# Regrouping linear attention so that the values are never formed, with half the residual parked in DRAM

## The chip, the cores and the metric

The kernel runs on one core of a Trainium2 chip. Of the engines named below, TensorE does the matmuls, and VectorE, ScalarE and GpSimd the work element by element; SBUF and PSUM are memories on the chip, and matmuls write to PSUM. The metric is the device time of one execution in microseconds (us), the lowest being best. Every time below is a median of several executions. Ratios are the mean time of one kernel's runs over that of the other kernel's runs in the same rounds, so a ratio isn't quite the ratio of the medians quoted beside it. The kernel before moved between 1643.9 and 1644.4 us from one set of rounds to the next; differences below half a microsecond between sets are therefore not read.

## The reference, cut to what matters

Four layers on 2048 tokens of width 1024: attention, feed-forward, attention, feed-forward, each with a layer norm in front and a residual around it. The attention is linear, with 32 heads of 32:

```python
q, k, v = ...                                  # slices of layernorm(x) @ wqkv, per head
phi = lambda t: jnp.where(t > 0, t + 1, jnp.exp(t)) + 1e-6
pq, pk = phi(q), phi(k)
kv  = jnp.einsum("bhsd,bhse->bhde", pk, v)     # summed over all 2048 tokens
z   = jnp.einsum("bhsd->bhd", pk)
num = jnp.einsum("bhqd,bhde->bhqe", pq, kv)
den = jnp.einsum("bhqd,bhd->bhq", pq, z)[..., None] + 1e-6
return (num / den) @ wo
```

The feed-forward layers (width 3584, relu(gate) times up, then down) are most of the time and aren't changed.

## The kernel before: the parts concerned

Tokens are 16 tiles of 128, in four quarters of four tiles. A "unit" is one projection of one token tile onto 512 columns: eight matmuls into one of four PSUM buffers. Whatever has to happen some units later is put on a list (`later.at(n, f)`), which `tick()` works off after each unit; in two stretches the order of the instructions on VectorE, ScalarE or GpSimd is exactly the order in which they are written (`manual_schedule`).

```python
def phi(self, ps, out):                        # keys: 1 ScalarE pass, 2 VectorE instructions
    nc.scalar.activation(out=e, in_=ps, func=ACT.Exp)
    nc.vector.tensor_scalar(out=e, in0=e, scalar1=1.0, scalar2=1e-6, op0=ALU.min, op1=ALU.add)   # "min-and-add"
    nc.vector.scalar_tensor_tensor(out=out, in0=ps, scalar=0.0, in1=e, op0=ALU.max, op1=ALU.add) # "join"
# q_unit: queries instead take three ScalarE passes (Relu, Exp, + 1e-6) and the join

def kv_step(t):                                # kv += phi(K_t)^T V_t, per group of 4 heads
    for g in range(G):
        nc.tensor.matmul(kv[b][:, ...], lhsT=pk[t][:, g * P:(g + 1) * P],
                         rhs=va[t][:, g * P:(g + 1) * P], ...)

def z_mult(pq, sc, j):                         # denominator: a GpSimd product, then z_sum
    nc.gpsimd.tensor_tensor(out=prod, in0=pq, in1=zrow, op=ALU.mult); later.at(2, z_sum)
def z_sum(...):                                # VectorE: sum per head, + 1e-6, reciprocal; then z_scale
def z_scale(...):                              # GpSimd: phi(Q) times 1/den, then a DMA transpose

def fold_wo(i):                                # T = kv @ wo, 16 single matmuls of 512 columns
    ps = ...                                   # even i: 2 PSUM buffers, copied by VectorE
    nc.tensor.matmul(ps, lhsT=kvT[:, g, :], rhs=wo[:, g, :])
    (nc.scalar.activation if g % 2 else nc.vector.tensor_copy)(T[...], ps)
... (cut)
run(q2[:6])
run([with_fold(u, i) for i, u in enumerate(q2[6:] + q3[:6])])   # one unit, two folds, one unit, ...
```

Of the kernel before, what the change touches and what calls it, by code (L numbers as in the profile page):

```python
# [12 lines left out]
P = 128  # L13
NW = 512
HD = 32
QT = 4

# [61 lines left out]
class _Net:  # L79
    def __init__(self, tc, ctx, x_d, wqkv_d, wo_d, wg_d, wu_d, wd_d, out_d):  # L80
# [30 lines left out]
        self.kvp = pool("kvp", 1, space=PSUM)  # L111
        self.ring = _Ring(nc, self.wring, 5)
        self.later = _Later()

# [16 lines left out]
        self.xnT = {}  # L131
# [24 lines left out]
    def ln_norm(self, layer, t):  # L156
        nc = self.nc
        src = self.xb[t] if layer == 0 else self.x[t]
        stats = self.small.tile([P, 2, nc.vector.BN_STATS_DIM], F32, tag="stats")
        for c in range(2):  # L160
            self.ln_stat(t, src, c, stats)
        xn = self.ln_scale(src, *self.ln_rstd(stats))
        return xn

    def head(self):
# [10 lines left out]
        k0, k1, v0, v1 = (ring.place() for _ in range(4))  # L176
        self.load_x(0, 0)
        self.load_x(0, 1)
        v0(0, H)
        self.load_x(1)  # L180
        v0(H, 2 * H)
        self.load_x(2)
        v1()
        self.load_x(3)
        k0()
# [4 lines left out]
        k1()  # L190
        for t in range(8, self.ST):
            self.load_x(t)
        ring.load_to(5)
# [16 lines left out]
        with tc.manual_schedule(engines={mybir.EngineType.DVE, mybir.EngineType.Activation}):  # L210
            for j in range(QT):
                for c in range(2):
                    self.ln_stat(j, src[j], c, stats[j])
                r = self.ln_rstd(stats[j])
                xn = self.xnp.tile([P, self.D], BF16, tag="xn")
                for h in (0, 1) if j == 0 else (None,):
                    self.ln_scale(src[j], *r, xn, h)
                for h in range(2):
                    turn(j, xn, h)
# [9 lines left out]
    def ln_at(self, delay, layer, t, lag):  # L229
        def norm():  # L230
            xn = self.ln_norm(layer, t)
            self.later.at(lag, lambda: self.ln_turn(layer, t, xn))

        self.later.at(delay, norm)
# [5 lines left out]
    def phi(self, ps, out):  # L240
        nc = self.nc
        e = self.ep.tile([P, NW], F32, tag="e")
        nc.scalar.activation(out=e, in_=ps, func=ACT.Exp)  # L243
        nc.vector.tensor_scalar(out=e, in0=e, scalar1=1.0, scalar2=1e-6, op0=ALU.min, op1=ALU.add)  # L244
        nc.vector.scalar_tensor_tensor(out=out, in0=ps, scalar=0.0, in1=e,  # L245
                                       op0=ALU.max, op1=ALU.add)
# [7 lines left out]
    def plan_A(self, l):  # L254
        D = self.D
        cols = {"k0": D, "k1": D + NW, "v0": 2 * D, "v1": 2 * D + NW, "q0": 0, "q1": NW}
        for n in ("k0", "k1", "v0", "v1", "q0", "q1", "o0", "o1"):
# [6 lines left out]
    def layer_A(self, l, last_ln):  # L264
# [4 lines left out]
        pk, va, pq_of, pqT, T = {}, {}, {}, {}, []  # L269
# [4 lines left out]

        def slab_of(t):
            if t not in pk:
                s = self.slab.tile([P, 2, D], BF16, tag="slab", name=f"pkv{l}_{t}")
                pk[t], va[t] = s[:, 0, :], s[:, 1, :]
# [9 lines left out]
        def k_unit(q, j, c):  # L288
            t = q * QT + j
            slab_of(t)  # L290
            self.phi(project(f"k{c}", q, j), pk[t][:, c * NW:(c + 1) * NW])
            if c == H - 1:
                later.at(1, lambda: k_sum(t))

        def k_sum(t):
            if t == 0:
                nc.gpsimd.tensor_copy(out=ksum, in_=pk[t])  # L297
            else:
                nc.gpsimd.tensor_tensor(out=ksum, in0=ksum, in1=pk[t], op=ALU.add)  # L299

        def v_unit(q, j, c):
            t = q * QT + j
            slab_of(t)
            nc.scalar.activation(out=va[t][:, c * NW:(c + 1) * NW], in_=project(f"v{c}", q, j),
                                 func=ACT.Copy)

        def kv_step(t):

            for g in range(G):
                b, i = divmod(g, NW // P)  # L310
                nc.tensor.matmul(kv[b][:, i * P:(i + 1) * P], lhsT=pk[t][:, g * P:(g + 1) * P],  # L311
                                 rhs=va[t][:, g * P:(g + 1) * P], start=(t == 0 and i == 0),
                                 stop=(t == self.ST - 1 and i == NW // P - 1),
                                 skip_group_check=True)

        def z_row():

            hi = self.xnp.tile([P, D], BF16, tag="xn")
            nc.scalar.activation(out=hi, in_=ksum, func=ACT.Copy)
            for i in range(H):  # L320
                ps = self.ps3.tile([P, NW], F32, tag="b")
# [3 lines left out]

        def finish_kv():
            kvm = self.slab.tile([P, G, P], BF16, tag="slab", name=f"kvm{l}")
            for b in range(H):
                n = NW // P
                nc.vector.tensor_tensor(out=kvm[:, b * n:(b + 1) * n, :],  # L330
# [3 lines left out]
            nc.sync.dma_start_transpose(out=kvT, in_=kvm[:, :, :].rearrange("p g e -> p (g e)"))  # L334


        def q_unit(sc, j, c, lag):
            if j == 0 and c == 0:
                pqT[sc] = self.xnTp.tile([P, KT, QT * P], BF16, tag="xnT", name=f"pqT{l}_{sc}")
            if c == 0:  # L340
                pq_of[sc, j] = self.xnp.tile([P, D], BF16, tag="xn", name=f"pq{l}_{sc}_{j}")
            pq = pq_of[sc, j]
            ps = project(f"q{c}", sc, j)

            e = self.ep.tile([P, NW], F32, tag="e")
            nc.scalar.activation(out=e, in_=ps, func=ACT.Relu, scale=-1.0)  # L346
            nc.scalar.activation(out=e, in_=e, func=ACT.Exp, scale=-1.0)  # L347
            nc.scalar.activation(out=e, in_=e, func=ACT.Identity, bias=self.eps6[:, 0:1])  # L348
            nc.vector.scalar_tensor_tensor(out=pq[:, c * NW:(c + 1) * NW], in0=ps, scalar=0.0,  # L349
                                           in1=e, op0=ALU.max, op1=ALU.add)  # L350
            if c == H - 1:
                later.at(lag, lambda: z_mult(pq, sc, j))

        def z_mult(pq, sc, j):
            prod = self.prodp.tile([P, D], F32, tag="prod")
            nc.gpsimd.tensor_tensor(out=prod, in0=pq, in1=zrow, op=ALU.mult)  # L356
            later.at(2, lambda: z_sum(pq, prod, sc, j))

        def z_sum(pq, prod, sc, j):
# [4 lines left out]
            later.at(2, lambda: z_scale(pq, den, sc, j))  # L364

        def z_scale(pq, den, sc, j):
            nc.gpsimd.tensor_tensor(  # L367
                out=heads(pq), in0=heads(pq),
                in1=den[:, :].unsqueeze(2).to_broadcast([P, D // HD, HD]), op=ALU.mult)
            nc.sync.dma_start_transpose(out=pqT[sc][:, :, j * P:(j + 1) * P], in_=pq)  # L370
# [33 lines left out]
        def q_of(sc, lag):  # L404
            return [lambda j=j, c=c: q_unit(sc, j, c, lag) for j in range(QT) for c in range(H)]

        def out_of(sc):
            return [lambda j=j, c=c: out_unit(sc, j, c) for j in range(QT) for c in range(H)]

        def v_then_kv(q):  # L410
            u = column_major(v_unit, q)

            def last(j):
                u_j = u[QT + j]
                return lambda: (u_j(), later.at(2, lambda: kv_step(q * QT + j)))

            return u[:QT] + [last(j) for j in range(QT)]

        def k_then_kv(q):
            u = column_major(k_unit, q)  # L420

            def last(j):
                u_j = u[QT + j]
                return lambda: (u_j(), later.at(4, lambda: kv_step(q * QT + j)))

            return u[:QT] + [last(j) for j in range(QT)]
# [16 lines left out]
        first = column_major(v_unit, 0)  # L443
        if l == 0:

            first = [first[c * QT + j] for c, j in ((0, 0), (0, 1), (1, 0), (0, 2), (1, 1), (1, 2),
                                                    (0, 3), (1, 3))]
        def quarter0():
            run(first)
            run(k_then_kv(0))  # L450

        if l == 0:
            with self.tc.manual_schedule(engines={mybir.EngineType.DVE,mybir.EngineType.Activation}):
                quarter0()
        else:
            quarter0()
        run(column_major(v_unit, 1))
        run(k_then_kv(1))
        run(column_major(k_unit, 2))
        k3 = column_major(k_unit, 3)  # L460
        run(k3[:QT])
        ring.free_before((l, "k1"))
        run(k3[QT:])
        with self.tc.manual_schedule(engines={mybir.EngineType.DVE,mybir.EngineType.Pool}):
            ring.free_before((l, "v0"))
            later.at(5, z_row)
            run(q_of(0, 5), v_then_kv(2))
            run(q_of(1, 1), v_then_kv(3))
            ring.free_slowly((l, "q0"), later, 4)
            later.at(2, finish_kv)  # L470
            q2, q3, out0 = q_of(2, 1), q_of(3, 1), out_of(0)
# [4 lines left out]
            run(q2[:6])  # L476
            run([with_fold(u, i) for i, u in enumerate(q2[6:] + q3[:6])])
            run(q3[6:], out0[:2])
            run(out0[2:])
            ring.free_slowly((l, "o0"), later, 4)  # L480
            self.ln_later(last_ln, 0, 5, 4, 3)
            for sc in range(1, self.NQ):
                run(out_of(sc))
# [12 lines left out]
    def layer_B(self, l, final):  # L496
        nc, KT, D = self.nc, self.KT, self.D
        ring, later = self.ring, self.later
        for q in range(self.NQ):
# [22 lines left out]
            for n2 in range(D // NW):  # L522
# [6 lines left out]
                for dg in range(4):  # L529
                    ring.free_before((l, q, "d", n2, dg))  # L530
                    wd = ring.get((l, q, "d", n2, dg))
                    for j in range(QT):
# [3 lines left out]
                        for i, ps in enumerate(parts):  # L536
# [6 lines left out]
                            if dg == 3:  # L543
                                self.add_down(t, n2 * NW + i * n, ps[:, 0:n], final)
                        later.tick()
# [68 lines left out]
```

## Time and profile before

| | before |
|---|---|
| median | 1644.4 us |
| profiled span | 1642.1 us |
| TensorE waits, all rows | 5.6 us |
| of these, folding of wo | 1.5 us |
| kv matmuls (128 columns) | 256 |
| first projection, first gate of layer 2, first gate of layer 4 begin at | 7.49, 245.22, 1058.76 us |

TensorE works through nearly all of the span, so time is the number of matmuls times their spacing, plus holes. The views that show this stand in the prediction. One more: what VectorE does while wo is folded. Columns of a timeline are start, duration, engine, line, operation, output and inputs; in brackets the idle time before it and who ended it.

```profile
176.18 0.68 DVE L384 CAST T<-fold 128x512 bf16<-128x512 f32 x1
176.78 1.21 DVE L361 TENSOR_REDUCE den<-prod 128x32 f32<-128x1024 f32 x1
...
178.51 0.63 DVE L349 SCALAR_TENSOR_TENSOR pq<-ps,e 128x512 bf16<-128x512 f32 x1
179.06 0.68 DVE L384 CAST T<-fold 128x512 bf16<-128x512 f32 x1
```

And GpSimd in the same stretch:

```profile
175.22 1.92 POOL L367 TENSOR_TENSOR pq<-pq,den 128x1024 bf16<-128x1024 bf16 x1
178.07 2.13 POOL L356 TENSOR_TENSOR prod<-pq,zrow 128x1024 f32<-128x1024 bf16 x1 [0.93 <-DVE den L361]
```

### The profile page before, as it was taken

How to read it: one execution, taken by the hardware profiler on the slowest of the kernel's cores; microseconds unless marked ns; L12 is line 12 of the kernel's file. 1: busy time of each engine (PE TensorE's matmuls, PEld its weight loads, DVE VectorE, ACT ScalarE, POOL GpSimd, SP SyncE). 2: the span in 40 equal slices, each digit the busy share in tenths (PEclk: the TensorE clock that was granted, in tenths of full speed). 3: DMA queues.
4: the chain of work that ended last, by engine and by line, in shares of the span. 5: the costliest groups of instructions: out<-in, count | busy, mean ns of one | idle time of the engine just before them, and what ended most of it. 6: DMA issues, size and time to landing. Idle time of an engine off the chain costs nothing.

```text
span 1642.1 us, 18601 instructions
## 1 busy us (share of the span) xinstructions
PE 1625.1 (99%) x7632; PEld 749.7 (46%) x7786; DVE 577.7 (35%) x931; ACT 371.1 (23%) x699; POOL 195.6 (12%) x102
## 2 busy tenths in 40 slices
PE   8999999999999999999999999999999999999999
PEld 4444444444444444444444444444444444444444
DVE  6954876122211321222146457842112112211111
ACT  3356602101110110111033675121011101101110
POOL 0355800000000000000013566000000000000000
PEclk9999999999999999999999999999999999999999
DMA  8313726456445544644530146374544464455442
GB/s 251 57 52 82 180 41 172 148 168 191 154 137 169 156 151 157 187 150 138 168 76 1 58 104 154 56 201 145 176 144 153 159 198 150 144 158 163 154 160 71
DMA packets 298052, 227.18 MB, mean 138 GB/s; under 512 B 103152, under 2 KB 296048, under 8 KB 297968
## 3 DMA queue, kind: packets, MB, share of 16 engines
q1 hardware_dynamic: 293216, 221.80, 46.4%
q10 hardware_dynamic: 4752, 4.20, 0.8%
q8 instruction: 61, 1.00, 0.2%
q14 instruction: 23, 0.19, 0.0%
HBM read 197.13 MB, written 4.19 MB: 123 GB/s over the span
## 4 chain that ended last, share of the span: by engine, by line
PE 95%; ACT 2%; issue 1%; DVE 1%; DMA 1%; SPq 0%; ACTq 0%
PE pu L515 23%; PE pg L515 23%; PE acc L539 23%; PE ps L284 17%; PE ps L390 7%; PE kv L311 1%; DMA x<-in_A_x_dram 1%; ACT e L347 1%; ACT e L346 1%; PE acc_last L539 0%; DVE den L361 0%; ACT e L348 0%; DVE pq L349 0%; PE fold L378 0%; SPq L251 0%
## 5 line engine op out<-in xcount | busy, mean ns | idle before, releaser
L515 PEld LDWEIGHTS <-t 128*128 128x128 bf16 x3584 | 350.5, 98 | 423.1
L515 PE MATMUL pu<-xnT,t 128*128 128x512 bf16 x1756 | 420.2, 379 | 2.0
L515 PE MATMUL pg<-xnT,t 128*128 128x512 bf16 x1756 | 419.9, 379 | 1.7
L539 PE MATMUL acc<-t,hT 128*128 128x512 bf16 x1728 | 380.6, 379 | 2.0
L521 DVE TENSOR_TENSOR hT<-pu,rg 128x512 bf16<-128x512 f32 x224 | 154.7, 690 | 572.0 <-PE pu L515 553.5
L284 PE MATMUL ps<-t,xnT 128*128 128x512 bf16 x1500 | 338.1, 379 | 2.4 <-DVE xnT L206 0.3
L520 ACT ACTIVATE rg<-pg 128x512 f32<-128x512 f32 x224 | 133.6, 596 | 737.5 <-PE pg L515 708.8
L539 PEld LDWEIGHTS <-hT 128*128 128x128 bf16 x1820 | 177.9, 98 | 209.1
L284 PEld LDWEIGHTS <-xnT 128*128 128x128 bf16 x1536 | 148.6, 98 | 174.9 <-issue 1.6
L390 PE MATMUL ps<-T,pqT 128*128 128x512 bf16 x502 | 110.6, 379 | 0.5
L143 ACT ACTIVATE rstd<-mv,eps 128x1 f32<-128x1 f32 x64 | 18.8, 294 | 344.0 <-DVE mv L141 344.0
L297 POOL CAST ksum<-pkv 128x1024 f32<-128x1024 bf16 x2 | 2.1, 1036 | 682.3 <-DVE pkv L245 682.3
L554 DVE TENSOR_TENSOR xo<-x,acc 128x512 bf16<-128x512 f32 x31 | 21.3, 688 | 170.0 <-PE acc L539 170.0
L136 DVE BATCH_NORM_STATS2 stats<-x 128x6 f32<-128x512 f32 (+1 forms) x120 | 78.2, 672 | 1.8 <-DMA x<-in_A_x_dram 1.1
L390 PEld LDWEIGHTS <-pqT 128*128 128x128 bf16 x512 | 50.1, 98 | 60.4
L356 POOL TENSOR_TENSOR prod<-pq,zrow 128x1024 f32<-128x1024 bf16 x32 | 68.0, 2126 | 58.2 <-DVE den L361 35.8
L551 DVE TENSOR_TENSOR x<-x,acc 128x512 f32<-128x512 f32 x32 | 21.7, 677 | 149.5 <-PE acc L539 148.4
L299 POOL TENSOR_TENSOR ksum<-ksum,pkv 128x1024 f32<-128x1024 f32 x30 | 65.0, 2167 | 69.6 <-DVE pkv L245 68.2
L244 DVE TENSOR_SCALAR e<-e 128x512 f32<-128x512 f32 x64 | 54.6, 853 | 40.8 <-ACT e L243 40.8
L349 DVE SCALAR_TENSOR_TENSOR pq<-ps,e 128x512 bf16<-128x512 f32 x64 | 42.9, 670 | 68.3 <-ACT e L348 68.2
L367 POOL TENSOR_TENSOR pq<-pq,den 128x1024 bf16<-128x1024 bf16 x32 | 61.2, 1912 | 10.5 <-issue 4.0
L243 ACT ACTIVATE e<-ps 128x512 f32<-128x512 f32 x64 | 37.7, 596 | 66.4 <-PE ps L284 65.3
(46 smaller groups left out, 490.1 us busy)
## 6 DMA issues: line engine op xcount, KB each, us to landing
t<-in_B_W_gate_dram SPq DMA_DIRECT2D x56, 1024.0 KB, 6.5
t<-in_B_W_up_dram SPq DMA_DIRECT2D x56, 1024.0 KB, 5.3
t<-in_B_W_down_dram SPq DMA_DIRECT2D x64, 896.0 KB, 5.1
t<-in_A_wqkv_dram SPq DMA_DIRECT2D x11, 1024.0 KB, 5.1
t<-in_A_wo_dram SPq DMA_DIRECT2D x4, 1024.0 KB, 5.1
out_dram<-xo ACTq DMA_DIRECT2D x31, 128.0 KB, 2.2
x<-in_A_x_dram SPq DMA_DIRECT2D x15, 256.0 KB, 8.0
t<-in_A_wqkv_dram SPq DMA_DIRECT2D x2, 512.0 KB, 4.9
```

The source lines that it names most:

```text
L136: self.nc.vector.bn_stats(out=stats[:, c, :], in_=src[:, c * fmax:(c + 1) * fmax])
L244: nc.vector.tensor_scalar(out=e, in0=e, scalar1=1.0, scalar2=1e-6, op0=ALU.min, op1=ALU.add)
L284: nc.tensor.matmul(ps, lhsT=self.xnT[l, l_q][:, kt, j * P:(j + 1) * P], rhs=w[:, kt, :], start=(kt == 0), stop=(kt == KT - 1))
L299: nc.gpsimd.tensor_tensor(out=ksum, in0=ksum, in1=pk[t], op=ALU.add)
L349: nc.vector.scalar_tensor_tensor(out=pq[:, c * NW:(c + 1) * NW], in0=ps, scalar=0.0, in1=e, op0=ALU.max, op1=ALU.add)
L356: nc.gpsimd.tensor_tensor(out=prod, in0=pq, in1=zrow, op=ALU.mult)
L367: nc.gpsimd.tensor_tensor(out=heads(pq), in0=heads(pq), in1=den[:, :].unsqueeze(2).to_broadcast([P, D // HD, HD]), op=ALU.mult)
L390: nc.tensor.matmul(ps, lhsT=pqT[sc][:, g, j * P:(j + 1) * P], rhs=T[g // 2][:, g % 2, n2 * NW:(n2 + 1) * NW], start=(g == 0), stop=(g == G ...
L515: nc.tensor.matmul(ps, lhsT=w[:, kt, fi * P:(fi + 1) * P], rhs=self.xnT[l, q][:, kt, :], start=(kt == 0), stop=(kt == KT - 1))
L520: nc.scalar.activation(out=rg, in_=pg, func=ACT.Relu)
L521: nc.vector.tensor_tensor(out=h[:, fi, :], in0=pu, in1=rg, op=ALU.mult)
L539: nc.tensor.matmul(ps[:, 0:n], lhsT=hT[ft // 4][:, ft % 4, j * P:(j + 1) * P], rhs=wd[:, k, i * n:(i + 1) * n], start=(ft == 0), stop=(ft ...
```

## The change

The intent: phi(K)^T V = (phi(K)^T xn) Wv, where xn are the normed tokens. First xn^T phi(K) is summed over all tokens (the same number of matmuls as the V projection), then it is multiplied with the value weights, which takes half as many kv matmuls as before. All normed tokens and all phi(K) must then be in SBUF together; in the third layer room for them is made by sending half the residual to DRAM in layer 2 and fetching it back after the products. The core of the diff:

```diff
-        def kv_step(t):
-            for g in range(G):
-                nc.tensor.matmul(kv..., lhsT=pk[t][...], rhs=va[t][...])       # 16 tiles x 8
+        def m_units(d):                              # d: block of the model dimension
+            for h in range(H):
+                for t in range(self.ST):
+                    nc.tensor.matmul(ps, lhsT=self.xn[l, t][:, d * P:(d + 1) * P],
+                                     rhs=self.pk[l, t][:, h * NW:(h + 1) * NW], ...)
+                nc.scalar.activation(out=mt[...], in_=ps, func=ACT.Copy)
+        def kv_step(d, mt):
+            for g in range(G):
+                nc.tensor.matmul(kv..., lhsT=Wv[:, d, ...], rhs=mt[...])       # 8 blocks x 8
-            nc.sync.dma_start_transpose(out=kvT, in_=kvm)                      # no longer needed
+        # queries of the last quarter: phi of kind "v" (Exp on ScalarE, min-and-add and join on VectorE)
+            self.phi(project(f"q{c}", sc, j), pq[...], KINDS[...] if sc < 3 else "v")
+            for i in range(self.ST - QT):            # denominators of 12 tiles beside the products
+                later.at(ZR + 2 + i * 5 // 2, lambda i=i: z_mult(*divmod(i, QT)))
+            for d in range(KT): m_units(d)
+            if l > 0: later.at(1, lambda: [self.bring_back(t) for t in range(self.NS)])
+            run(q3[:3])
+            run([with_fold(u, i) for i, u in enumerate(q3[3:] + out0[:3])])
+        # layer 2, as each of token tiles 0 to 7 is finished:
+            self.send_away(t)
... (cut: layer norm in two parts, homes of xn and phi(K), key and query units in turn, order of weights)
```

## The prediction

> **What bounds the kernel now.** I read the page first (busy shares, slices, chain), then TensorE's waits, then its groups by form, then short timelines. The page:
>
> ```profile
> PE 1625.1 (99%) x7632; PEld 749.7 (46%) x7786; DVE 577.7 (35%) x931; ACT 371.1 (23%) x699; POOL 195.6 (12%) x102
> PE   8999999999999999999999999999999999999999
> DVE  6954876122211321222146457842112112211111
> PE 95%; ACT 2%; issue 1%; DVE 1%; DMA 1%; SPq 0%; ACTq 0%
> ```
>
> TensorE is busy in every slice and makes 95% of the chain that ended last. VectorE is dense only in the two attention layers (the first six slices and the twenties), which are the ones the change rewrites. A busy engine can still hide gaps, so next comes who made TensorE wait (total us, times, longest):
>
> ```profile
> PE idle L174 <- DVE zero L171: 2.1, 1, 2.1
> PE tp L203 <- DVE xn L152: 1.7, 2, 1.3
> PE fold L378 <- DVE T L384: 1.5, 4, 0.4
> PE ps L284 <- DVE xnT L206: 0.3, 1, 0.3
> ```
>
> All its waits sum to 5.6 us: the start and the folding of wo. So the time is matmuls times spacing. Durations of single matmuls are modelled and overlap; the spacing comes from starts in a timeline:
>
> ```profile
> 151.27 0.61 PE L311 MATMUL kv<-pkv 128*128 128x128 bf16 x8
> 151.71 3.62 PE L284 MATMUL ps<-t,xnT 128*128 128x512 bf16 x16
> 155.17 0.61 PE L311 MATMUL kv<-pkv 128*128 128x128 bf16 x8
> ```
>
> Sixteen matmuls of 512 columns take 155.17 - 151.71 = 3.46 us, 216 ns each (8 of them, one "unit", 1.73 us); eight of 128 columns take 0.44 us, 55 ns each. The kv group counts 256:
>
> ```profile
> L311 PE MATMUL kv<-pkv 128*128 128x128 bf16 x256 | 19.5, 219 | 0.1
> ```
>
> Last, VectorE beside GpSimd, because the change gives VectorE more work per unit at the start (start, duration):
>
> ```profile
> 879.80 1.98 DVE L244 TENSOR_SCALAR e<-e 128x512 f32<-128x512 f32 x1 [0.57 <-ACT e L243]
> 881.81 0.69 DVE L245 SCALAR_TENSOR_TENSOR pkv<-ps,e 128x512 bf16<-128x512 f32 x1
> 882.42 0.42 DVE L244 TENSOR_SCALAR e<-e 128x512 f32<-128x512 f32 x1
> 882.87 0.69 DVE L245 SCALAR_TENSOR_TENSOR pkv<-ps,e 128x512 bf16<-128x512 f32 x1
> 883.48 1.63 DVE L244 TENSOR_SCALAR e<-e 128x512 f32<-128x512 f32 x1
> ```
>
> The same min-and-add takes 0.42 us or up to 1.98 us; the long ones lie beside GpSimd's running key sum (2.17 us each), while the join between them stays at 0.69.
>
> **What the Trainium skill says.** "TensorE: Matmul & The Clock Gate", Part 1, "Wait — 56ns, not 53.3ns?", gives warm start-to-start spacings of 55.6 ns at 128 columns and 215.7 ns at 512; the trace agrees (55 and 216). "SBUF — State Buffer", "Who interferes with whom", says that a tensor_scalar in a two-port mode and a GpSimd instruction lock each other out for a whole instruction, and that a VectorE instruction with one SBUF input outside those modes does not contend; the trace agrees (0.42 against 1.63 to 1.98, joins constant). "DMA: Bandwidth & Descriptors", "Issuing engines are not separate DMA queues", says all transfers share 16 engines, so the new traffic queues among the weights; the page has that DMA share at 0.4 to 0.6 in the feed-forward layers, which leaves room.
>
> **The change part by part.** kv = phi(K)^T V is regrouped as (xn^T phi(K))^T Wv.
>
> 1. Removed: the V projection, 16 tiles x 2 halves x 8 = 256 matmuls of 512 columns per layer. Added: xn^T phi(K), 8 blocks x 2 halves x 16 tiles = 256 of 512. Net zero on TensorE. This is why a large rewrite buys little.
>
> 2. kv itself: the sum ran over 16 token tiles, it now runs over 8 blocks of the model dimension, eight matmuls of 128 columns each: 64 instead of 128 per layer. The compiled orders confirm it: 256 before, 128 after, and 7786 against 7658 matmuls in all, every other class unchanged. 128 x 0.055 = 7.1 us off the path, since TensorE is the path.
>
> 3. kv comes out already transposed: one DMA transpose per layer and its wait go. TensorE did not wait for it (no such row above): nothing directly.
>
> 4. The folding of wo: in the last token quarter phi(Q) changes from three ScalarE passes (0.59 + 0.63 + 0.72 = 1.94 us, more than the 1.73 us of a unit) to one ScalarE pass and one more VectorE pass, and most of q is finished earlier. ScalarE and VectorE were both behind there before, hence 1.5 us of waits (about 2.1 us of holes counting the restart, from starts). Per fold unit TensorE now takes 1.73 + 2 x 0.216 = 2.16 us, ScalarE 0.6 + 0.59, VectorE 0.42 + 0.69 + 0.68 plus two denominator reductions (1.7 us each) in the first few: over five units 9.0 + 3.4 = 12.4 against 10.8. The slack of two fold buffers (4.3 us) covers 1.6. I count -1.5 us for the two layers.
>
> 5. The start, first layer. Keys and queries come first instead of values and keys. VectorE rows by the compiled order between the first key join and the end of the layer norms of quarter 1 (14 joins, 8 scalings, 7 aggregates, 12 statistics, 6 min-adds): by duration 9.7 + 4.4 + 1.4 + 7.7 + 2.6 = 25.8 us; instructions follow each other about 0.07 us closer than their durations say, so some 22.5 to 23. TensorE's 14 units are 24.2 us. VectorE is almost full, but keeps up; the lag it may build up is covered by four PSUM buffers, about 5.2 us less the 1.8 us of a normal phi. The order places statistics behind each key join that starts a key sum, so the lock should bite rarely. In the first quarter eight query units in a row cost ScalarE 1.94 against 1.73, a drift of 0.2 per unit, 1.7 us in all, again within the slack. On the other side, the hole of 1.3 us in front of the fourth token tile was an order effect (a statistic of a later tile that waited for its load stood before the aggregate), and the new order is better there. I net this to +1 us, between -1 and +4.
>
> 6. From the last keys to xn^T phi(K): the first product needs the last key tile only as its 16th matmul, 3.2 us in; phi is then done (0.6 + 0.42 + 0.69 plus one lock of 1.5 is 3.2). 0 to +1 us for both layers, taken as 0.
>
> 7. The residual: 8 tiles of 512 KB leave in the second layer, at the end of token quarters 0 and 1, and return in the third. 8.4 MB on top of 227 MB. Out: the next layer norm writes into a tile that left, so VectorE, in order, waits for the third store. From 1 MB in 5.1 us (median to landing of weights) I estimate about 2 us per tile behind one weight load: landed 10 to 11 us after the last down block starts. The multiplication behind it is first missed when the gate-up PSUM pair runs out, some 14.7 us after it (6.0 us of down block plus 8.6). Slack about 4 us, twice. Back: the first four are issued as the products end, then the second half of wo, which the ninth fold needs some 14 us later; 2 MB plus 1 MB at that rate is 12 to 15 us less a head start of 3. Hidden. Taken as +0.3 in all.
>
> Sum: -7.1 - 1.5 + 1 + 0 + 0.3 = -7.3 us, so 1637 us. GpSimd gets denser beside the products (2.13 + 1.91 = 4.0 us per query tile at one per 4.3 us), but nothing needs its last tiles before the third output quarter, two quarters later.
>
> **Rivals.**
> (a) VectorE becomes the bound in the first layer's key-query stretch. For: the full 25.8 us by durations, the lock, and that layer norm ran there before at 90% busy already (44.87 of 50 us in the window from 50 to 100). Against: in that window TensorE was still busy 49.74 of 50, and the third layer has its norms done before its keys begin. It would cost 3 to 8 us and take back the gain: 1640 to 1645.
> (b) The stores hold up VectorE in the second layer, or the returning tiles hold up wo in the third. For: one queue in order, and waits of VectorE on DMA in the compiled order. Against: slack of 4 us and more. It would cost 2 to 10 us: 1639 to 1647.
> (c) All holes go: the start improves by 1 to 2 us and the folds by 2.1. Then 1633 to 1635.
>
> **Range and chances.** The arithmetic term 7.1 is certain within 0.3 us, if spacing holds. The rest is -3 to +5, skewed to the slow side. I predict 1637 us, 1634 to 1641.5 for 8 in 10. 2% is 33 us; nothing above reaches that on either side: faster 0.01, same 0.98, slower 0.01.
>
> **What would show it.** Step 1: 512 matmuls of the new product, spaced 216 ns, in place of the V units. Step 2: 128 kv matmuls. Step 4: the fold row of TensorE's waits near zero. Step 5: no new wait of ps on phi's join between 20 and 110 us, and the products beginning about 97 us after the first unit. Step 7: no wait of TensorE on hT at the two quarter changes of the second layer, none of fold on the wo load in the third. The prediction is wrong if TensorE's waits sum to more than 10 us, or if its spacing is not 216 ns where two operands that are both token tiles are multiplied.

## The result, and the profile after

| | before | after | difference |
|---|---|---|---|
| median of the same rounds | 1644.4 us | 1641.03 us | -3.4 us |
| ratio (95%) | | 0.998 (0.9962 to 0.9997) | |
| profiled span | 1642.1 us | 1639.1 us | -3.0 us |
| first projection begins | 7.49 us | 7.14 us | -0.35 us |
| first projection to first gate of layer 2 | 237.73 us | 237.01 us | -0.7 us |
| third layer (825.38 and 824.31 us) to first gate of layer 4 | 233.38 us | 231.47 us | -1.9 us |

The time lies in the predicted range, but of the predicted gain of 7.3 us only 3.4 arrived. The stages between sum to the whole: -0.35 - 0.7 - 1.9 = -2.95 us, so the two feed-forward layers took what they took before. The page of the changed kernel, busy time and chain:

```profile
PE 1617.8 (99%) x7506; PEld 742.7 (45%) x7658; DVE 576.8 (35%) x947; ACT 332.6 (20%) x635; POOL 194.7 (12%) x102
PE 83%; DVE 1%; issue 1%; ACT 0%; ACTq 0%
```

TensorE is still the engine that sets the end. (The chain's listed shares add up to 85% here and to 100% before, so the two chains are not compared.) The new kv row has half the count of before:

```profile
L402 PE MATMUL kv<-mt,t 128*128 128x128 bf16 x128 | 9.8, 219 | 0.0
```

The new product, in a timeline of TensorE:

```profile
155.65 7.07 PE L389 MATMUL ps<-slab,x 128*128 128x512 bf16 x31
162.55 0.61 PE L402 MATMUL kv<-mt,t 128*128 128x128 bf16 x8
```

Two sums of 16 matmuls take 162.55 - 155.65 = 6.90 us, 216 ns each (one of the 32 records is missing). Neither count nor spacing is off. What is off is who made TensorE wait (total us, times, longest):

```profile
PE fold L460 <- DVE T L466: 4.5, 4, 1.2
...
PE ps L355 <- DVE slab L316: 1.3, 1, 1.3
PE ps L355 <- DVE xnT L261: 1.0, 2, 0.7
PE ps L472 <- DVE T L466: 0.6, 2, 0.3
PE ps L355 <- DMA t<-in_A_wqkv_dram: 0.5, 1, 0.5
```

The row that was to vanish, fold on the copies of T, has grown from 1.5 to 4.5 us, and with 0.6 us of output projections waiting for the same copies it is 5.1 us. All rows, with the three left out above (2.1, 0.3 and 0.2 us), sum to 10.5 us against 5.6 before, which passes the 10 us at which the prediction called itself wrong. Here is TensorE in the first layer's fold window:

```profile
178.12 1.89 PE L355 MATMUL ps<-t,xnT 128*128 128x512 bf16 x7
181.24 0.59 PE L460 MATMUL fold<-t,kvT 128*128 128x512 bf16 x2 [1.23 <-DVE T L466]
...
184.57 0.59 PE L460 MATMUL fold<-t,kvT 128*128 128x512 bf16 x2 [1.01 <-DVE T L466]
```

VectorE, which copies the even folds, in the same window:

```profile
175.85 1.97 DVE L305 TENSOR_SCALAR e<-e 128x512 f32<-128x512 f32 x1
177.85 0.69 DVE L316 SCALAR_TENSOR_TENSOR pq<-ps,e 128x512 bf16<-128x512 f32 x1
178.46 1.41 DVE L305 TENSOR_SCALAR e<-e 128x512 f32<-128x512 f32 x1
...
180.51 0.68 DVE L466 CAST T<-fold 128x512 bf16<-128x512 f32 x1
181.11 1.21 DVE L440 TENSOR_REDUCE den<-prod 128x32 f32<-128x1024 f32 x1
...
183.84 0.68 DVE L466 CAST T<-fold 128x512 bf16<-128x512 f32 x1
```

And GpSimd:

```profile
175.41 2.12 POOL L435 TENSOR_TENSOR prod<-pq,zrow 128x1024 f32<-128x1024 bf16 x1 [12.78 <-DVE den L440]
177.49 2.10 POOL L447 TENSOR_TENSOR pq<-pq,den 128x1024 bf16<-128x1024 bf16 x1
183.06 1.91 POOL L447 TENSOR_TENSOR pq<-pq,den 128x1024 bf16<-128x1024 bf16 x1 [3.48 <-DVE den L442]
```

Read the three together. The first pair of folds was finished by about 176.1; its copy came at 180.51, after two units of phi whose min-and-adds took 1.97 and 1.41 us instead of 0.42. They end 0.3 us after GpSimd's product and 0.3 us after its scaling. The third pair of folds needs the buffer and waits 1.23 us. Then a denominator reduction and another phi stand before the next copy, and the fourth pair waits 1.01 us. The third layer repeats it to a hundredth (1.23 and 1.01). Two causes offer themselves, the lock by GpSimd and plain VectorE work in a fixed order; the trace alone does not part them.

The other new hole lies in the first quarter of the first layer: a min-and-add, the GpSimd key sums that it fell into, and the projection behind it. VectorE:

```profile
26.83 2.03 DVE L305 TENSOR_SCALAR e<-e 128x512 f32<-128x512 f32 x1 [0.53 <-ACT e L304]
```

GpSimd:

```profile
24.13 4.44 POOL L371 TENSOR_TENSOR ksum<-ksum,slab 128x1024 f32<-128x1024 f32 x2 [2.42 <-DVE slab L316]
```

TensorE:

```profile
29.51 13.97 PE L355 MATMUL ps<-t,xnT 128*128 128x512 bf16 x63 [1.27 <-DVE slab L316]
```

### The profile page after: what moved, and what is told of

Its sections match the earlier page's. It is cut to its first block, busy times and chain, and to the rows that moved or that the text cites. A ratio compares the mean times of both kernels' runs of the same rounds, so it can differ in the third digit from the quotient of the medians. Undisturbed runs are those within 1.5% of the kernel's fastest.

```text
span 1639.1 us, 18247 instructions
## 1 busy us (share of the span) xinstructions
PE 1617.8 (99%) x7506; PEld 742.7 (45%) x7658; DVE 576.8 (35%) x947; ACT 332.6 (20%) x635; POOL 194.7 (12%) x102
## 4 chain that ended last, share of the span: by engine, by line
PE 83%; DVE 1%; issue 1%; ACT 0%; ACTq 0%
PE acc L605 23%; PE pu L581 23%; PE pg L581 23%; PE ps L355 6%; PE ps L389 3%; PE ps L472 3%; PE acc_last L605 0%; DVE e L305 0%; PE kv L402 0%; DVE T L466 0%; DVE den L440 0%; DVE pq L316 0%; PE fold L460 0%; DVE kvT L414 0%; DVE den L442 0%
## 5 line engine op out<-in xcount | busy, mean ns | idle before, releaser
L355 PE MATMUL ps<-t,xnT 128*128 128x512 bf16 x1002 | 223.0, 379 | 4.2 <-DVE slab L316 1.3
L355 PEld LDWEIGHTS <-xnT 128*128 128x128 bf16 x1024 | 99.8, 98 | 123.5 <-issue 3.2
L371 POOL TENSOR_TENSOR ksum<-ksum,slab 128x1024 f32<-128x1024 f32 x23 | 49.2, 2140 | 86.8 <-DVE slab L316 76.8
L305 DVE TENSOR_SCALAR e<-e 128x512 f32<-128x512 f32 x80 | 49.2, 615 | 28.5 <-ACT e L304 28.4
L440 DVE TENSOR_REDUCE den<-prod 128x32 f32<-128x1024 f32 x32 | 38.9, 1216 | 49.9 <-POOL prod L435 49.9
```

The source lines that it names most:

```text
L355: nc.tensor.matmul(ps, lhsT=self.xnT[l, l_q][:, kt, j * P:(j + 1) * P], rhs=w[:, kt, :], start=(kt == 0), stop=(kt == KT - 1))
L371: nc.gpsimd.tensor_tensor(out=ksum, in0=ksum, in1=pk, op=ALU.add)
```

## The experiments

All are edits of the changed kernel, and all gave the right result (within the comparison's tolerance) except where it is said. The theory: VectorE, which works in order, is too late with the copies of T in the last token quarter. Under it lie two claims: (A) what makes it late is the lock between the min-and-adds and GpSimd, (B) it is the sum of plain VectorE work there. Rival (C) is that ScalarE is the worse bound, so that its three passes would cost more still; a rival (D), that the denominator chains don't matter to the folds, is told apart with their run. One kernel tests the arithmetic term.

### The arithmetic term: every kv matmul twice

```diff
-            memset(mask, 1.0)
+            memset(mask, 0.5)
-            for g in range(G):
+            for g, r in [(g, r) for g in range(G) for r in range(2)]:
```

> The changed kernel with every kv matmul issued twice and the mask at 0.5, so the result is the same: 256 matmuls of 128 columns again, as before the change. If step 2 of the prediction holds (55 ns each, on the path), +7.1 us: 1647.5 to 1648.7 us. If they were hidden, 1641.

Measured: 1647.82 us, 6.8 us more than the changed kernel (ratio to before 1.0025). The count doubles and nothing else moves:

```profile
L402 PE MATMUL kv<-mt,t 128*128 128x128 bf16 x256 | 16.9, 219 | 0.0
```

128 kv matmuls are worth 6.8 us on the path (7.2 if each kernel is set against the kernel before in its own rounds). The term of 7.1 us was real, so about 4 us of it were given back elsewhere.

### phi of the last quarter as in the kernel before

```diff
-            self.phi(..., KINDS[...] if sc < 3 else "v")
+            self.phi(..., KINDS[...] if sc < 3 else "s")     # three ScalarE passes, no min-and-add
```

> The changed kernel, but the last token quarter computes phi as the kernel before did (three ScalarE passes, VectorE only joins). A: no min-add, so no lock; the holes fall to about those of before (1.06 us per layer) or less, 1636.5 to 1638.5 us. B: less VectorE work, the same. Rival C (ScalarE, at 1.94 us plus a copy of 0.6 per 2.16 us unit, is the worse bound, which is why the change left it): 1641 to 1645 us.

Measured: 1636.76 us, 4.3 us less than the changed kernel; the fold row is 0.6 us and that of the output projections 0.3. So ScalarE's three passes are not worse here: claim C falls. That one choice of the change, which the prediction had counted as a gain, is worth as much as the whole miss of 3.9 us. It removes lock and VectorE work together, so A and B stay.

### phi of the last quarter with the minimum taken straight from PSUM

```diff
+        elif kind == "n":
+            nc.vector.tensor_scalar(out=e, in0=ps, scalar1=0.0, scalar2=None, op0=ALU.min)
+            nc.scalar.activation(out=e, in_=e, func=ACT.Exp)
```

> The changed kernel (1641.03 us), but in the last token quarter VectorE takes min(x,0) straight from PSUM (about 0.69 us, no lock with GpSimd) and ScalarE the exponential of it, in place of ScalarE's exponential and VectorE's min-add out of SBUF (0.42 us alone). VectorE gets more work per unit, the lock goes. Theory A (the lock between min-add and GpSimd makes the holes of about 3.0 us per layer in front of the folds): holes shrink to under 1 us per layer, 1636 to 1638.5 us. Rival B (VectorE simply has too much work there): six units cost 0.27 us more each, holes grow, 1642 to 1645 us.

Measured: 1641.30 us, nearly the changed kernel. The lock is gone (each minimum takes 0.63 to 0.69 us), but the holes moved: 3.7 us of output projections waiting for a join, 1.1 us of folds. The reason stands on VectorE:

```profile
178.73 0.68 DVE L308 TENSOR_SCALAR e<-ps 128x512 f32<-128x512 f32 x1
180.17 0.69 DVE L322 SCALAR_TENSOR_TENSOR pq<-ps,e 128x512 bf16<-128x512 f32 x1 [0.76 <-ACT e L309]
```

The join follows its own minimum in VectorE's order, so VectorE stands still for 0.76 us each time while ScalarE takes the exponential. The run put a serial chain where the lock had been, and the compiler also set TensorE's folds one at a time among the matmuls of the units, so it tells A and B apart not at all: a failed experiment.

### The same order with a min-and-add of another form

```diff
-            nc.vector.tensor_scalar(out=e, in0=e, scalar1=1.0, scalar2=1e-6, op0=ALU.min, op1=ALU.add)
+            nc.vector.scalar_tensor_tensor(out=e, in0=e, scalar=1.0, in1=eps6.to_broadcast([P, NW]),
+                                           op0=ALU.min, op1=ALU.add)        # last quarter only
```

> Only the form of the min-and-add in the last token quarter changes: instead of a tensor_scalar (0.42 us alone, 1.97, 1.41, 0.82 and 1.03 beside GpSimd) a scalar_tensor_tensor with the small constant as a broadcast second input, about 0.69 us, which should not be held by GpSimd. Same order, same engines, same dependencies, same GpSimd work and the same two denominator reductions. Theory 'lock': the stretched instructions lose about 3.5 us of lock per layer and gain 8 x 0.27 = 2.2 us of plain work, of which the part in front of the second copy of folded wo shrinks by 1.4 us; TensorE's waits of fold fall from 4.5 to under 2 us in all and the kernel ends at 1637 to 1639. Theory 'amount of VectorE work' (reductions and one more pass, the lock not needed): more VectorE work, so the fold waits stay at 4.5 or grow and the kernel ends at 1641 to 1643.

Measured: 1642.86 us, fold waits 5.2 us. That agrees with "amount of work", but the run's own premise is false:

```profile
176.25 2.23 DVE L309 SCALAR_TENSOR_TENSOR e<-e,eps 128x512 f32<-128x512 f32 x1
178.51 0.69 DVE L321 SCALAR_TENSOR_TENSOR pq<-ps,e 128x512 bf16<-128x512 f32 x1
```

The same operation takes 2.23 us with two SBUF inputs and 0.69 with one input in PSUM. The Trainium skill says so ("SBUF — State Buffer", "Who interferes with whom": an instruction with two SBUF inputs contends with a GpSimd instruction that reads SBUF); I had read the half of that passage that speaks of one input. So the lock stayed and work was added, and both theories expect a slower kernel. It refutes the expectation under "lock" as I wrote it, not the lock. Nor was the order the same throughout: from the fourth pair on the folds stand one at a time among the units here too.

### Denominator chains every two steps: GpSimd and reductions leave the window

```diff
-                later.at(ZR + 2 + i * 5 // 2, lambda i=i: z_mult(*divmod(i, QT)))
+                later.at(ZR + 2 + i * 2, lambda i=i: z_mult(*divmod(i, QT)))
```

> The changed kernel, but the denominator chains of the first three query quarters are emitted every 2 steps in place of every 2.5, so that GpSimd's last products and scalings and VectorE's last two reductions fall before the folds. A and B both: the holes in front of the folds go, -5 to -6 us, 1635 to 1636.5 us. If the holes came from the order of the copies alone (rival D), no change: 1640.5 to 1641.5 us.

Measured: 1634.82 us (ratio to before 0.9944), 0.2 us below the range expected, and the fold rows are gone. The first two copies of VectorE now come in time:

```profile
178.50 0.68 DVE L466 CAST T<-fold 128x512 bf16<-128x512 f32 x1
...
180.15 0.68 DVE L466 CAST T<-fold 128x512 bf16<-128x512 f32 x1
```

Rival D falls: the folds are the same, only their neighbours left. And an edit of a few characters is worth 6 us, more than the change itself. What left the window was two reductions of VectorE and three GpSimd instructions (a product and two scalings, about 2 us each); the next three kernels put back the like of them, one kind at a time and together.

### Two unused reductions put back, then three unused GpSimd products, then both

```diff
+            # in the version above; z_red and z_both: after the 2nd and the 4th unit of the last quarter
+            nc.vector.tensor_reduce(out=den, in_=heads(zrow), op=ALU.add) ; + 1e-6 ; reciprocal
+            # z_lock and z_both: three times after the 2nd unit
+            nc.gpsimd.tensor_tensor(out=prod, in0=pq_of[3, 0], in1=zrow, op=ALU.mult)
```

Reductions alone:

> The version with the denominator chains every two steps (1634.8, no fold waits), with two unused denominator reductions (1.21 + 0.18 + 0.35 us each, same input size, no GpSimd work with them) put back into VectorE's order where the changed kernel has its own two, one before and one after the first fold. Theory 'lock': the added 3.5 us of VectorE work per layer fit into the slack of two fold buffers, so the time stays at 1634.5 to 1636. Theory 'amount of work': the fold waits come back, 1638 to 1641. Theory 'both needed': 1635.5 to 1638.

Measured: 1636.48 us, +1.7. The expectation of "both needed" holds. TensorE's wait row:

```profile
PE fold L460 <- DVE T L466: 1.4, 2, 0.7
```

GpSimd alone:

> The version with the denominator chains every two steps, with three unused GpSimd products (about 2.1 us each, in a row, then the usual one) put into the last token quarter and no VectorE work added. Theory 'lock': the min-and-adds of the quarter wait out these products, fold waits return and the time is 1637 to 1641. Theory 'amount of VectorE work': GpSimd's ops alone do nothing, 1634.5 to 1635.5.

Measured: 1636.22 us, +1.4, less than the lock theory's 1637 and more than the other's 1635.5: a miss for both in their pure form. The min-and-adds are stretched to 1.99, 1.62, 1.02 and 1.02 us, about as in the changed kernel, and still little is seen of it: TensorE's fold row is 0.6 us.

Both together:

> Both additions of the two runs before in one kernel: denominator chains every two steps, plus two unused reductions in VectorE's order plus three unused GpSimd products in the last token quarter. Theory 'one queue against a fixed slack': VectorE's extra time before the second copy of folded wo adds up (reductions 3.5 us, lock some 3 us, per layer) and only what passes the slack of two fold buffers is seen, so the two together cost clearly more than the 1.7 and 1.4 us of each alone: 1639 to 1641.5, back at the time of the changed kernel, with 3 to 5 us of fold waits. Rival 'independent costs' : 1634.8 + 1.7 + 1.4 = 1637.9, within 0.5, and something else in the changed kernel makes up the rest.

Measured: 1642.46 us, +7.6 over the version without either, against 1.7 + 1.4 = 3.1 for the sum of the two. It is 1 us above the range expected (probably because the three added products and the usual one make four in a row, where the changed kernel has two and two), and clearly not the 1637.9 of independent costs. TensorE's wait row:

```profile
PE fold L460 <- DVE T L466: 5.0, 2, 2.5
```

The row shows only one hole per layer; the second is hidden by something else. After each hole of 2.52 us TensorE's granted clock in this profile was 0.50 for about 3 us: the eight matmuls from 182.00 us took 3.09 us, not 1.73, and the fourth pair of folds began at 185.09 us. VectorE's second copy ended only at 184.84, so at full clock that pair would have waited about 1.1 us instead. The slow stretch therefore adds little: the two executions with a mean clock of 0.998 and 0.999 took 1642.6 and 1642.7 us, the two with 1.000 took 1642.1 and 1642.3.

This settles A and B: neither alone. VectorE has the slack of two fold buffers. The reductions eat most of it, or the lock does, and each alone shows about 1.5 us; once both are there, everything further is paid in full. "Alone" has a limit: the version that they start from keeps one GpSimd product in the window, which stretches one VectorE instruction there (a min-and-add to 1.99 us, and with the reductions added the + 1e-6 to 1.08). Not tested is the direct remedy, the copies of T earlier in VectorE's order.

### The first quarter of the first layer

Here too the scalar_tensor_tensor form was tried first (keys of the first quarter), with the same false premise:

> The changed kernel with the scalar_tensor_tensor form of the min-and-add for the keys of the first layer's first token quarter alone (8 instructions, about 0.69 instead of 0.42 us each, not held by GpSimd). Theory 'lock' for the 1.3 us wait of a key projection on a join near 28 us: that wait falls below 0.3 and the time to 1639.5 to 1640.2. Rival, VectorE is simply full there (the rival that the prediction called (a)): 2.2 us more work make that wait longer or move it, 1641 to 1643.

Measured: 1642.06 us; two of these instructions took 1.12 and 2.29 us beside GpSimd. The lock stayed, work was added; nothing is told apart. Next, two ScalarE passes and no min-and-add, for all eight key units:

```diff
+        elif kind == "t":
+            nc.scalar.activation(out=e, in_=ps, func=ACT.Relu, scale=-1.0)
+            nc.scalar.activation(out=e, in_=e, func=ACT.Exp, scale=-1.0)       # the 1e-6 left out
```

> The keys of the first layer's first token quarter with two ScalarE passes (the second input's minimum is then not needed and the 1e-6 left out), no min-and-add on VectorE. The scalar_tensor_tensor form was itself held by GpSimd (2.29 us), so that run did not remove the lock; this one does. Theory 'lock and its collision near 27 us': the 1.3 us wait of a projection on a join goes, 1639.1 to 1639.8. Rival, the hole comes from the loads and the order of the layer norms: 1640.5 to 1641.5.

Measured: 1640.09 us, a gain of 0.5 to 0.9 us, depending on the set of rounds compared with, between the two expectations. The wait on the join is gone, but the hole has moved to the third token tile. VectorE, at the join in front of that tile's normalization:

```profile
14.12 0.69 DVE L322 SCALAR_TENSOR_TENSOR slab<-ps,e 128x512 bf16<-128x512 f32 x1 [1.42 <-ACT e L312]
```

The second ScalarE pass makes this join late, and the normalization that stands behind it in VectorE's fixed order starts at 14.73 instead of 13.16 us. So only tiles 2 and 3 were switched, whose keys come after GpSimd's sums begin; the changed kernel ran again in the same rounds as their baseline.

```diff
-            self.phi(..., KINDS[l // 2][min(q, 1)][c])
+            self.phi(..., "v" if t < 2 and l == 0 else KINDS[l // 2][min(q, 1)][c])    # KINDS "t" for quarter 0
```

> Keys of tiles 0 and 1 of the first layer as in the changed kernel (their min-and-adds, 0.43 us each, come before GpSimd's first key sum), those of tiles 2 and 3 with two ScalarE passes and no min-and-add. Theory 'lock': the layer norms of the first four tiles stay where they are, the 1.3 us wait on a join near 28 us goes and nothing replaces it, 1.2 to 1.8 us less than the changed kernel of the same rounds. Rival, the quarter's layer norms and loads set the pace: the hole moves again and the gain is under 0.8 us.

> The changed kernel once more, unchanged, as the baseline of these rounds: 1640.5 to 1641.5.

Measured: 1638.82 us against 1640.83 us for the changed kernel: 2.0 us less, a little more than expected under "lock" (some of it is the start, whose waits for loads differ by half a microsecond from run to run). TensorE no longer stops:

```profile
18.09 13.11 PE L361 MATMUL ps<-t,xnT 128*128 128x512 bf16 x60
```

The lock itself is still there, on one of the min-and-adds kept (0.86 us) and now on a normalization (2.27 instead of 0.53 us), where no wait of TensorE follows. So the cause of the hole near 28 us was the min-and-add behind the key sums. The run takes its plain work away with its lock; that the lock was the larger part is read from the trace (2.03 us, of which 0.41 is plain work), not shown by a run of its own.

### The residual kept on the chip

```diff
-                            self.send_away(t)
+                            pass
-                later.at(1, lambda: [self.bring_back(t) for t in range(self.NS)])
+                pass
```

> The changed kernel without the stores of eight residual tiles and without their return; the result is wrong on purpose. My reading of the trace: the transfers are hidden, 1640.7 to 1641.4. Rival (b) of the prediction, stores or returning tiles hold something up: 1637 to 1640.

The result is wrong (relative error 0.51). Measured: 1640.76 us (1640.41 to 1641.20), 0.1 to 0.3 us below the changed kernel's two medians, which is not clear of noise. No cost of storing and returning 8.4 MB is seen.

### The versions that beat both

> The candidate that should beat both: denominator chains every two steps, and every phi with two ScalarE passes and one VectorE join (no min-and-add anywhere, the 1e-6 left out). If what is left over the count of matmuls is the fold window and the lock in the first quarter, 1632.5 to 1634. If ScalarE's 1.2 us per unit in place of 0.6 sets a new wait, 1634.5 to 1637.

Measured: 1634.02 us, at the upper edge: the first quarter has the moved hole of the run above.

> All findings together: denominator chains every two steps, two ScalarE passes and no min-and-add everywhere except the keys of tiles 0 and 1 of the first layer. 0.8 to 1.5 us less than the all-two-pass version (1634.0), so 1632.5 to 1633.5; if the start is set by loads, no gain over it.

Measured: 1633.25 us (1632.73 to 1633.62; ratio to before 0.9934, 95% 0.9921 to 0.9948), 0.8 us less than the version before it and 10.7 us less than the kernel before. TensorE's waits are then 3.6 us, all of them at the start. This version leaves out the 1e-6 in phi; whoever wants the same arithmetic takes the denominator chains every two steps alone, 1634.8 us.

## Why the prediction was right or wrong

**The range held, the gain did not.** Predicted -7.3 us, measured -3.4.

**Steps 1, 2 and 3 were right.** The product is spaced 216 ns like any other, the kv matmuls went from 256 to 128, and doubling them cost 6.8 us for the 7.1 counted. (For step 3 there is only the trace: no row of TensorE's waits names the transpose, before or after.)

**Step 4, the folding of wo, failed, with the wrong sign.** It said: "VectorE 0.42 + 0.69 + 0.68 plus two denominator reductions ... 12.4 against 10.8. The slack of two fold buffers (4.3 us) covers 1.6. I count -1.5 us for the two layers." The reductions were counted, the slack was counted, but the min-and-add was entered with its undisturbed 0.42 us, although GpSimd works through the same window and although the prediction itself showed 1.98 us for this instruction. The five min-and-adds from 175.85 to 187.53 us took 1.97 + 1.41 + 0.36 + 0.82 + 1.03 = 5.59 us instead of 2.1, so VectorE was 5.1 us behind over the five units (1.6 + 3.5), not 1.6, and 4.3 us of slack do not cover it. A sum over five units is too coarse besides, since each copy has its own deadline: the third pair of folds needed its buffer at 179.85 us (178.12 + 1.73), and the copy that frees it ended at 181.19. The two min-and-adds before it lost 2.5 us; without this loss it would have ended near 178.7, in time (an estimate from these lines). Fold and output waits came to 5.1 us where 0 was predicted. The runs with reductions alone, products alone and both (+1.7, +1.4, +7.6) show just this: the slack hides either, not both. Put in time: spacing the denominator chains more closely saves 6.2 us and leaves no fold wait, and the holes of the kernel before, restarts included (a hole between starts is some 0.16 us longer than the wait in its row), were 2.1 us, so this step made +4.1 us where -1.5 was written.

**Step 5, the start, came out near its sum for a wrong reason.** "The lock should bite rarely" was false in effect: the stretched min-and-add made the new 1.3 us wait on a join near 28 us that this step had ruled out, and with tiles 2 and 3 switched the way from the fourth tile's first projection to the first product is 1.8 us shorter (89.17 instead of 90.97 us). The loads and the order of the first tiles gave about as much back: the first projection began 0.35 us earlier, and the hole of 1.3 us before the fourth tile went, as the step said. Its sign "the products beginning about 97 us after the first unit" missed too: it was 102.2 us (109.37 - 7.14), since 97 is the 56 units alone, without the holes and the transposes of the first tiles. For the size of steps 5 to 7 together: with the fold trouble gone the kernel is 9.2 us faster than before in the same rounds; the kv matmuls account for 7.1 and the fold holes of the kernel before, restarts included, for 2.1. Nothing clear of noise is left, where +1.3 was predicted.

**Step 6** needs no correction: no new wait of TensorE appears where the products begin. **Step 7** was right: taking the transfers away changed nothing clear of noise, and no wait of a fold on its weights appeared.

**Of the rivals,** (a) named the right mechanism, VectorE with the lock, in the first layer's key-query stretch and its band of 1640 to 1645 held the result; but two thirds of the loss (4.1 us against 1.8) lie in the last quarter of both attention layers, where (a) didn't look. (b) fell with the run without transfers. (c) came true only in the versions of the experiments.

## What to carry to other kernels

When a change moves an instruction to another stage, price it with the duration it has beside its new neighbours; a VectorE instruction that GpSimd can lock out has two prices, here 0.42 us and up to 2. A buffer's slack can hide most of either of two delays and not both together, so test suspected causes together as well as singly: here 1.7 and 1.4 us alone became 7.6. And before rewriting arithmetic, look at when side work is issued: spacing the denominator chains by two steps instead of two and a half gave 6 us, where halving the kv matmuls had kept 3.4 of its 7.

## What the Trainium skill lacked or had wrong

- "TensorE: Matmul & The Clock Gate", Part 2, "Back-to-back issue gap", gives about 131 ns per 512-column matmul and about 81 ns per 128-column matmul for a sustained stream of weight loads and matmuls. Here, with a weight load for every matmul, they are 216 ns (6.90 us for 32) and 55 ns; the figures that the page calls isolated are the ones that held, and using 81 would have mis-sized the main term by half.
- "SBUF — State Buffer", "Who interferes with whom", was right on each form that ran: the min-and-add as a tensor_scalar on SBUF 0.36 to 2.36 us, scalar_tensor_tensor with two SBUF inputs 0.63 to 2.29 us, the same with one input in PSUM 0.63 to 0.69, tensor_reduce 1.21. It says "for the whole instruction"; what it lacks is an example of what that means for a tiny one: the + 1e-6 on 128x32 took 1.08 instead of 0.18 us beside a GpSimd product in the run with reductions alone.
- I found no page that has what a detour through another engine costs in a fixed order: VectorE's minimum, ScalarE's exponential and VectorE's join left VectorE idle for 0.76 us per unit, of which the exponential itself is 0.6.
